# Attention and a gated layer on one core: the decay of the first 320 tokens summed by itself, its rows sent ahead of the weights, copies of the preparation given to planned engines, the last tile's end in parts

## The chip, the cores and the metric

One core of one Trainium2 chip. The time is that of the whole program on the device in microseconds (us). The program uses TensorE (PE, matmuls and transposes), ScalarE (ACT), VectorE (DVE), GpSimd (POOL), and SyncE (SP), whose queue issues all DMA transfers.

## The reference

Attention with a forget-gate decay over 8 batches, 8 heads, 576 tokens and a head width of 64, then a layer over the 4608 tokens (512 wide, 1024 inside), all in float32:

```python
scores = scale * np.matmul(q, k.transpose(0, 1, 3, 2))
log_f = np.log(np.clip(f, 0.0001, 1.0))
cum = np.cumsum(log_f, axis=-1)
decay = cum[:, :, :, None] - cum[:, :, None, :]
scores = np.where(causal, -1000000000.0, scores + decay)
attn = np.exp(scores - max); attn = attn / (sum + 1e-09)
x = np.matmul(attn, v)                  # heads side by side: 4608 x 512

h = x @ w_in                            # 512 -> 1024
solu = h * softmax(h)
mu, var = mean(solu), var(solu)
ln = (solu - mu) / np.sqrt(var + 1e-06) * g_ln
out = ln @ w_out                        # 1024 -> 512
```

## The kernel before

Every step is an `op` with an engine, an assumed duration in ns, a due time, a function that emits the instructions, and the keys that it reads and writes. `Plan.schedule` lays all steps out on a clock of its own. On each engine it takes, among the steps that could start within `WAIT` ns of the earliest one, the one that is due first. The instructions are emitted in that order, so every engine's queue has a fixed order. A due time only ranks steps. On that clock a transfer of `kb` takes `kb / 0.25` ns of the wire and ends at `max(t + 1900, wire + 1300)`; eight may be in flight, and one issue takes 620 ns of SyncE.

Where the planner expects TensorE to have nothing to do for over 200 ns before 140 us, the program emits filler matmuls (L742), whose result nobody reads:

```python
for _ in range(int(FILL * (t - busy - 100.0) / (256 * COLUMN))):   # FILL 1.2, COLUMN 0.4525
    nc.tensor.matmul(dst[:, :256], blank[:, :P], blank, start=True, stop=True)
```

Here `t` is where the next step of TensorE is expected and `busy` where the last ended, 3200 ns at the start.

**Attention.** Heads are taken in 32 pairs (8 batches of 4). A pair has five query tiles (64, then 4 x 128 tokens). For each tile and head `scores` multiplies q and k into PSUM, VectorE subtracts the mask and takes the maximum (L508), ScalarE takes the exponential with its sum (L511), VectorE inverts the sums (L519, L520), GpSimd scales (L524), `transposes` turns the tiles on TensorE (L550) and ScalarE copies them to SBUF (L555); `values` multiplies by v (L590). Matmuls run on operands split into a high and a low float32r part. Only the first batch's first 320 tokens ("early" or "native": half 0 of pairs 0 to 3) use plain float32: q and k are loaded as they are, and one row more holds the decay's sums, sent by DMA from `c32`, a piece of tile p_4 (`kz_k<-p`, `ks_k<-p`). Their outputs go from PSUM to `xt` by one ScalarE copy (L608).

**The decay.** f (64 rows of 576) is loaded into tile e, clipped (L298), its logarithm taken (L299), summed by a scan into tile z (L305) and copied into `c32` (L306 to L311). The keys of these copies are called `summed`; loads of pairs 1 to 3, the rows themselves and w_in's chunks 1 to 3 read `summed`, so they are issued behind them. Step L301 loads ScalarE's table for the exponential (due -40). For all other pairs the sums go split in two through DRAM (`c_scratch`, due `C_OUT`).

**Weights.** w_in and w_out come packed in four chunks of 1 MB each. `weights` loads one into a buffer that is still free, unpacks it with ScalarE (L351, L357) and VectorE (L360, L362) into e, z or ptl, and `prepare_w_in` and `prepare_w_out` then make high and low parts: wi_h on ScalarE (L372), wi_l on GpSimd (L373), w_out times g_ln on ScalarE (L389) and its low part on VectorE (L391).

**The layer.** `layer(n)` takes 128 tokens: split x (L624, L625), 24 matmuls by w_in into hps (L629 to L631), maximum (L638), exponential (L639), the weighing and mean (L643 to L646), the square with its sum on ScalarE (L648) and the centring on GpSimd (L652), which both write z; 8 transposes (L665), high and low parts (L667, L668), 24 matmuls by w_out into one bank (L676 to L678), an output copy (L685) and a transfer. The last tile is like the others.

## Time and profile before

| | |
|---|---|
| time, median of 3 runs | 815.35 us (815.05 to 815.91) |
| the profiled execution | 815.81 us, its span 814.0 us |
| TensorE busy | 799.7 us (98%), 4973 matmuls and transposes |
| VectorE busy | 580.6 us (71%) |
| ScalarE busy | 556.7 us (68%) |
| GpSimd busy | 457.3 us (56%) |
| moved by DMA | 106.96 MB, mean 131 GB/s |

Busy times are shares of the span of one execution. Matmuls are pipelined, and the filler matmuls count as busy too, so TensorE's 98% is not work of the reference alone. Due times and the planner's clock are no measured times.

### The profile page before, as it was taken

To read this page: it belongs to the slowest core of one execution; us is meant where nothing else is said; L and a number is where in the kernel's file an instruction comes from. 1 tells how busy PE (TensorE), PEld (TensorE's weight loads), DVE (VectorE), ACT (ScalarE), POOL (GpSimd) and SP (SyncE) were. 2 spreads that over 40 slices of the span, in tenths; PEclk is the share of its full clock that TensorE was granted. 3 is DMA by queue.
4 is the path that set the end of the run, shared out by engine and by line. 5 is a ranking of instruction groups with operands and counts; after the bars stand their busy time and mean duration, and the time that the engine had idled before them with its cause. 6 is when DMAs were issued, how large, how long until landed. Compare 5 with 4: busy or idle time off the path is not lost.

```text
span 814.0 us, 16055 instructions
## 1 busy us (share of the span) xinstructions
PE 799.7 (98%) x4973; PEld 677.2 (83%) x4973; DVE 580.6 (71%) x1847; ACT 556.7 (68%) x1386; POOL 457.3 (56%) x668
## 2 busy tenths in 40 slices
PE   8999999999999999999999999999999999999997
PEld 6767888888888888888888888888888888888885
DVE  3669888897777777777777777777877777764322
ACT  4977777887666776777777777767767776764332
POOL 5466677766656564666665555656654655432320
PEclk9999999999999999999999999999999999999999
DMA  8658778787554445555554445555444554000000
GB/s 300 164 133 246 185 184 204 211 198 182 144 139 111 125 108 133 148 145 137 153 131 110 111 118 148 145 136 142 125 121 125 132 128 100 28 14 14 26 27 26
DMA packets 64069, 106.96 MB, mean 131 GB/s; under 512 B 11184, under 2 KB 25520, under 8 KB 63216
## 3 DMA queue, kind: packets, MB, share of 16 engines
q1 hardware_dynamic: 63984, 105.95, 49.7%
q8 instruction: 39, 0.64, 0.3%
q14 instruction: 46, 0.38, 0.2%
HBM read 39.11 MB, written 10.03 MB: 60 GB/s over the span
## 4 chain that ended last, share of the span: by engine, by line
PE 87%; DVE 7%; ACT 1%; issue 1%; POOL 1%; DMA 1%; SPq 0%; DVEq 0%; POOLq 0%; ACTq 0%
PE ps_o L590 13%; PE ps_t L550 10%; PE ps_o L676 8%; PE hps L629 8%; PE ps_o L677 7%; PE ps_o L678 7%; PE hps L631 7%; PE hps L630 7%; PE ps L503 5%; PE ps L504 5%; PE ps_t L665 3%; PE ps L742 3%; DVE p L508 2%; PE ps_o L742 1%; PE ps L501 1%
## 5 line engine op out<-in xcount | busy, mean ns | idle before, releaser
L524 POOL TENSOR_SCALAR p<-p,ri 64x64 f32<-64x64 f32 (+4 forms) x320 | 170.3, 547 | 138.1 <-DVE ri L520 108.1
L511 ACT ACTIVATE p<-p,nm 128x192 f32<-128x192 f32 (+4 forms) x320 | 179.3, 561 | 77.5 <-DVE nm L508 62.9
L558 DVE TENSOR_TENSOR ptl_f32r<-ps_t,pth_f32r 128x384 fp32r<-128x384 f32 (+3 forms) x272 | 138.2, 519 | 39.5 <-ACT pth_f32r L555 37.9
L508 DVE CUSTOM_DVE_ANT_0 p<-ps,mask 128x192 f32<-128x192 f32 (+4 forms) x320 | 132.2, 424 | 44.9 <-PE ps L504 28.0
L555 ACT CAST pth_f32r<-ps_t 128x384 fp32r<-128x384 f32 (+3 forms) x272 | 119.1, 450 | 44.4 <-PE ps_t L550 40.5
L550 PE MATMUL ps_t<-ident,p 128*128 128x128 f32 x800 | 129.9, 274 | 2.4 <-DVE ptl_f32r L558 1.1
L676 PE MATMUL ps_o<-wo_f32r,zh 128*128 128x512 f32 x288 | 121.8, 423 | 0.3 <-ACT zh L667 0.3
L629 PE MATMUL hps<-wi_h,xh 128*128 128x512 f32 x288 | 121.3, 421 | 0.4 <-DVE e L645 0.4
L550 PEld LDWEIGHTS ps_t<-ident,p 128*128 128x128 f32 x800 | 96.4, 140 | 28.5 <-POOL p L524 4.6
L677 PE MATMUL ps_o<-wo_f32r,zh 128*128 128x512 f32 x288 | 114.1, 396 | 0.0
L678 PE MATMUL ps_o<-wo_f32r,zl 128*128 128x512 f32 x288 | 113.7, 395 | 0.0
L631 PE MATMUL hps<-wi_h,xl 128*128 128x512 f32 x288 | 113.6, 394 | 0.0
L630 PE MATMUL hps<-wi_l,xh 128*128 128x512 f32 x288 | 113.6, 394 | 0.0
L503 PE MATMUL ps<-ks_f32r,qs_f32r 128*64 128x64 f32 (+2 forms) x360 | 110.6, 314 | 2.2 <-DVE nm L508 1.9
L504 PE MATMUL ps<-kz_f32r,qz 128*64 128x64 f32 (+2 forms) x360 | 103.7, 295 | 0.0
L590 PE MATMUL ps_o<-pth_f32r,vs_f32r 128*128 128x256 f32 (+1 forms) x368 | 93.7, 267 | 0.0
L652 POOL TENSOR_SCALAR z<-e,st 128x1024 f32<-128x1024 f32 x36 | 42.7, 1185 | 73.5 <-ACT z L648 73.3
L668 DVE TENSOR_TENSOR zl<-ps_t,zh 128x512 fp32r<-128x512 f32 x72 | 47.6, 687 | 50.8 <-ACT zh L667 50.4
L625 POOL TENSOR_TENSOR xl<-xt,xh 128x512 fp32r<-128x512 f32 x36 | 46.5, 1292 | 63.4 <-ACT xh L624 63.1
L503 PEld LDWEIGHTS ps<-ks_f32r,qs_f32r 128*128 128x128 f32 (+1 forms) x360 | 64.8, 180 | 13.8 <-DVE nm L508 6.9
L590 PE MATMUL ps_o<-ptl_f32r,vs_f32r 128*64 128x256 f32 (+1 forms) x368 | 72.0, 262 | 0.0
L590 PEld LDWEIGHTS ps_o<-pth_f32r,vs_f32r 128*128 128x128 f32 x368 | 68.9, 188 | 1.5
(110 smaller groups left out, 1608.6 us busy)
## 6 DMA issues: line engine op xcount, KB each, us to landing
raw<-in_qk_dram SPq DMA_DIRECT2D x64, 288.0 KB
ks_f32r<-hi SPq DMA_DIRECT2D x128, 144.0 KB
raw<-in_v_dram SPq DMA_DIRECT2D x32, 288.0 KB
kz_f32r<-raw SPq DMA_DIRECT2D x64, 144.0 KB
out_dram<-y SPq DMA_DIRECT2D x36, 256.0 KB
qs_f32r<-hi SPq DMA_DIRECT2D x56, 144.0 KB
qs_f32r<-raw SPq DMA_DIRECT2D x56, 144.0 KB
qz<-hi SPq DMA_DIRECT2D x56, 80.0 KB
```

What stands on the lines that cost most here:

```text
L503: nc.tensor.matmul(dst, qs(p)[:, h, q0:q0 + nq], ks(p)[:, h, cols], start=True, stop=False)
L508: op(DVE, R_NS[i], at + 0.5, lambda a=a, e=e, key=key: nc.vector.tensor_tensor_reduce(pr[:, a:e], ps[plan.place[key]][:nq, :e - a], mask[: ...
L511: op(ACT, E_NS[i], at + 1.3, lambda: nc.scalar.activation(pr, pr, AF.Exp, bias=x, scale=-1.0, accum_out=sm[m][i][:nq, h, 0:1]), [("nm", m, ...
L524: op(POOL, N_NS[i], at + 2.8, lambda g=g, pg=pg: nc.gpsimd.tensor_scalar(pg, pg, r_[:, g:g + 1], 1.0, ALU.mult, ALU.mult), [("ri", m, i)], ...
L550: nc.tensor.transpose(tp[:, s, :], pt[i][:, k * P:(k + 1) * P], ident)
L590: nc.tensor.matmul(o[:mm, a:w], vv, mv, start=(j == 0 and x == 0), stop=(j == order[-1] and x == 0))
L629: nc.tensor.matmul(hps[:, sl], xh[:, c, :], wi_h[:, c, sl], start=(c == 0), stop=False)
L630: nc.tensor.matmul(hps[:, sl], xh[:, c, :], wi_l[:, c, sl], start=False, stop=False)
L631: nc.tensor.matmul(hps[:, sl], xl[:, c, :], wi_h[:, c, sl], start=False, stop=(c == NCC - 1))
L676: nc.tensor.matmul(o, zh[a][:, j], wo(0, k), start=(k == 0), stop=False)
L677: nc.tensor.matmul(o, zh[a][:, j], wo(1, k), start=False, stop=False)
L678: nc.tensor.matmul(o, zl[a][:, j], wo(0, k), start=False, stop=(k == NFC - 1))
```

## The change

- The clip and the logarithm run in two pieces, tokens 0 to 319 and 320 to 575. A scan of the first piece into tile y fills `c32`; the scan of all 576 tokens into z follows (due -30) for `c_scratch`.
- w_in's chunk 0 is due at -98, right after f. w_out's chunks read `summed`, so they are issued behind the rows' copies.
- A helper `copied` puts a copy on an engine from a table: wi_h (all ScalarE), the product of w_out and g_ln (VectorE four, GpSimd two, ScalarE two), the transposed copies of the native pairs (VectorE for pair 1), their output copies (five of eight on VectorE). wi_l of chunk 2 goes to VectorE.
- The last tile: its square writes a part of p_4 and no longer z, VectorE does the centring in two halves of 512 columns, and the product by w_out runs in two halves of 256 columns with an output copy and a transfer each, the four low-part matmuls of a group behind the eight high-part ones.
- New due times, `WAIT` from (30, 90, 60, 180, 30) to (0, 90, 60, 60, 0) for (PE, ACT, DVE, POOL, SP).

```diff
+WI_H, WI_L, WO_H, WO_L = (1, 1, 1, 1), (3, 3, 2, 3), (2, 3, 2, 2, 3, 1, 1, 2), (2, 2, 2, 2, 2, 2, 2, 2)
+P_32, X_32 = (1, 2, 1, 1), (2, 2, 2, 2, 1, 1, 1, 2)
-WAIT = (30.0, 90.0, 60.0, 180.0, 30.0)
+WAIT = (0.0, 90.0, 60.0, 60.0, 0.0)
-PAIR = 23.6
-C_OUT = 19.0
-START = 89.0
-HALF = ((4.2, 1.6), (34.8, -12.5))
-W_IN, W_OUT, LOAD = (8.2, 2.2), (39.4, 2.1), (6.8, 5.2)
-W_DMA = (-1.8, 1.6)
+PAIR = 23.79
+C_OUT = 24.8
+START = 89.4
+HALF = ((3.1, 1.8), (29.8, -13.0))
+W_IN, W_OUT, LOAD = (8.4, 2.1), (28.9, 4.9), (8.9, 6.4)
+W_DMA = (3.2, 0.5)
-FIRST = 107.8
-STAGES = (5.2, 5.4, 2.7, 19.0, 10.3)
+FIRST = 106.0
+STAGES = (6.6, 3.8, 2.5, 19.8, 10.3)
...
+    def copied(eng, ns, due, out_, in_, reads, writes, scale=1.0, clear=(), port=True):
+
+        def fn():
+            if eng == ACT:
+                nc.scalar.activation(now(out_), now(in_), AF.Copy, scale=scale)
+            else:
+                (nc.vector if eng == DVE else nc.gpsimd).tensor_scalar(now(out_), now(in_), scale, 1.0, ALU.mult, ALU.mult)
+        op(eng, ns[eng], due, fn, reads, writes, clear=clear, port=port and eng == DVE)
...
-    op(DVE, 450, -99, lambda: nc.vector.tensor_scalar(ft, ft, 1.0e-4, 1.0, ALU.max, ALU.min), writes=[("e",)], port=True)
-    op(ACT, 800, -99, lambda: nc.scalar.activation(ft, ft, AF.Ln), writes=[("e",)])
-    op(ACT, 1500, -40, lambda: nc.scalar.activation(nhalf, ft[:, 0:1], AF.Exp), reads=[("e",)], writes=[("table",)])
+    for n, sl in enumerate((slice(0, HALF_S), slice(HALF_S, S))):
+        op(DVE, (330, 300)[n], -99 + n, lambda sl=sl: nc.vector.tensor_scalar(ft[:, sl], ft[:, sl], 1.0e-4, 1.0, ALU.max, ALU.min),
+           reads=[("e",)], writes=[("f", n)], port=True)
+        op(ACT, (560, 490)[n], -99 + n, lambda sl=sl: nc.scalar.activation(ft[:, sl], ft[:, sl], AF.Ln), reads=[("e",)], writes=[("f", n)])
+    op(ACT, 1500, -40, lambda: nc.scalar.activation(nhalf, ft[:, 0:1], AF.Exp), reads=[("e",), ("f", 0), ("f", 1)], writes=[("table",)])
...
-    op(DVE, 1380, -99, lambda: nc.vector.tensor_tensor_scan(zero, ft, zero, 0.0, ALU.add, ALU.add), reads=[("e",)], writes=[("z",)], port=True)
-    op(DVE, 300, -99, lambda: nc.vector.tensor_copy(c32[:, HALF_S:], zero[:H, :HALF_S]), reads=[("z",)], writes=[("p", 4)], port=True)
-    op(ACT, 260, -99, lambda: nc.scalar.copy(c32[:, 0:P], zero[:H, q_lo(2):q_lo(3)]), reads=[("z",)], writes=[("p", 4, "c")])
+    first = yt[:B * H, :HALF_S]
+    op(DVE, 830, -99, lambda: nc.vector.tensor_tensor_scan(first, ft[:, :HALF_S], zero[:, :HALF_S], 0.0, ALU.add, ALU.add),
+       reads=[("e",), ("f", 0), ("z",)], writes=[("y",)], port=True)
+    op(DVE, 1380, -30, lambda: nc.vector.tensor_tensor_scan(zero, ft, zero, 0.0, ALU.add, ALU.add),
+       reads=[("e",), ("f", 0), ("f", 1)], writes=[("z",)], port=True)
+    op(DVE, 300, -99, lambda: nc.vector.tensor_copy(c32[:, HALF_S:], first[:H]), reads=[("y",)], writes=[("p", 4)], port=True)
+    op(ACT, 260, -99, lambda: nc.scalar.copy(c32[:, 0:P], first[:H, q_lo(2):q_lo(3)]), reads=[("y",)], writes=[("p", 4, "c")])
...
-        dma(due + W_DMA[n // NCC], t, src..., reads=first, writes=tk)
+        dma(due + W_DMA[n // NCC] if n else -98, t, src..., reads=first, writes=tk)
...
-        op(ACT, 1050, due, lambda: nc.scalar.copy(wi_h[:, c, :], w), reads=[wk], writes=[("wi", c)])
-        op(POOL, 2360, due, lambda: nc.gpsimd.tensor_tensor(wi_l[:, c, :], w, wi_h[:, c, :].bitcast(F32), ALU.subtract),
-           reads=[wk, ("wi", c)], writes=[("wil", c)])
+        copied(WI_H[c], {ACT: 1050, DVE: 690, POOL: 1130}, due, wi_h[:, c, :], w, [wk], [("wi", c)])
+        op(WI_L[c], 2360 if WI_L[c] == POOL else 1170, due, lambda: (nc.gpsimd if WI_L[c] == POOL else nc.vector).tensor_tensor(
+            wi_l[:, c, :], w, wi_h[:, c, :].bitcast(F32), ALU.subtract), reads=[wk, ("wi", c)], writes=[("wil", c)], port=True)
...
-        weights(w_out[c], NCC + c, due, t, tk, w, wk)
+        weights(w_out[c], NCC + c, due, t, tk, w, wk, summed)
...
-            op(ACT, 600, due, lambda r=r, k=k: nc.scalar.activation(wo(0, k), w[:, r], AF.Copy, scale=g_sb[:, k:k + 1]),
-               reads=[("g",), wk], writes=[("wo", k)])
+            copied(WO_H[k], {ACT: 600, DVE: 400, POOL: 620}, due, lambda k=k: wo(0, k), w[:, r], [("g",), wk], [("wo", k)], scale=g_sb[:, k:k + 1])
...
-        op(ACT, 60 + 0.81 * n, at + 0.4, lambda: nc.scalar.copy(th(), ps_t[plan.place[key]][:, :cnt, :nq]),
-           [key], [("pth", i, g)], clear=to)
+        copied(P_32[p] if native else ACT, {ACT: 60 + 0.81 * n, DVE: 68 + 1.045 * n}, at + 0.4, th,
+               lambda: ps_t[plan.place[key]][:, :cnt, :nq], [key], [("pth", i, g)], clear=to, port=False)
...
-            op(ACT, 160 + 0.9 * w, at + 1.5, lambda: nc.scalar.copy(xo, ps_o[plan.place[key]][:D, :w]), [key], [(*xk, h)], clear=[xk])
+            copied(X_32[2 * p + h], {ACT: 160 + 0.9 * w, DVE: 68 + 1.045 * w}, at + 1.5, xo, lambda: ps_o[plan.place[key]][:D, :w],
+                   [key], [(*xk, h)], clear=[xk], port=False)
...
+        last = (n + 1) * P == NT
+        sq, sk = (pt[4][:, :DFF], ("p", 4)) if last else (zt, ("z",))
+        if last:
+            for a in range(2):
+                op(DVE, 360, at, lambda a=a: centre(nc.vector, slice(512 * a, 512 * a + 512)), [("e",), ("st", n % 2)], [("z", a)],
+                   clear=[("z",)], port=True)
+        else:
+            op(POOL, 1200, at, lambda: centre(nc.gpsimd), [("e",), ("st", n % 2)], [("z",)])
...
+        if last:
+            for b in range(2):
+                ok, cols = ("o", "y", n, b), slice(256 * b, 256 * b + 256)
+                ...
+                for a in range(2):
+                    for x in range(2):
+                        for k in range(4 * a, 4 * a + 4):
+                            op(PE, (2 - x) * 256 * COLUMN + 4, at + 3.0 * b + 0.1 * k, lambda k=k, x=x, product=product: product(k, x),
+                               [(("zh", "zl")[x], a), (("wo", k), ("wol", k))[x]] if x else [("zh", a), ("wo", k), ("wol", k)], [ok],
+                               take=ok if k == 0 and x == 0 else None)
+                op(ACT, 360, at + 3.0 * b, ...)            # y columns of this half
+                dma(at + 3.0 * b, out[n * P:(n + 1) * P, cols], yt[:, cols], 128, reads=[("y", b)])
+            return
```

The due times of the pairs' steps (`DUE` and `EARLY`) are new too; they have the same form.

## Rows read from the trace of the kernel before

**Rows 1.** Windows of one call; us and instructions of each engine busy

```profile
18.70:50.00 31.30, 31.30 (x205) 21.45 (x204) 18.50 (x82) 27.24 (x76) 17.65 (x26) 1.00 0.57 151
60.00:80.00 20.00, 18.85 (x128) 15.38 (x127) 19.29 (x43) 14.93 (x30) 12.31 (x15) 1.00 0.89 264
200.00:400.00 200.00, 199.69 (x1244) 173.12 (x1243) 150.87 (x500) 142.08 (x364) 121.24 (x174) 1.00 0.52 131
```

**Rows 2.** Windows of the filler matmuls (L742) alone

```profile
0.00:10.00 10.00, 6.58 (x45) 5.27 (x46) 1.00 0.62 204
10.00:18.70 8.70, 8.70 (x81) 7.63 (x79) 1.00 1.02 407
18.70:130.00 111.30, 31.13 (x242) 22.57 (x241) 1.00 0.70 186
```

**Rows 3.** Timeline 0 to 20 us: start, duration, instruction

```profile
0.72 0.57 SPq L289 DMA_DIRECT2D e<-in_f_dram  x1
...
3.39 0.62 DVE L298 TENSOR_SCALAR e<-e 64x576 f32<-64x576 f32 x1 [1.95 <-DMA e<-in_f_dram]
...
3.42 15.39 PE L742 MATMUL ps<-ident 128*128 128x256 bf16 x124 [3.42 <-POOL ident masks.py:199]
...
4.40 0.58 SPq L289 DMA_DIRECT2D wo_raw<-in_w_in_dram  x1
...
4.75 1.28 ACT L301 ACT_TABLE_LOAD   x1
...
5.03 0.43 SPq L289 DMA_DIRECT2D ptl_raw<-in_w_out_dram  x1
5.51 0.60 SPq L289 DMA_DIRECT2D xt<-in_w_out_dram  x1
...
6.15 0.29 ACT L307 COPY p<-z 8x128 f32<-8x128 f32 x1
...
6.79 1.24 SPq L289 DMA_DIRECT2D kz_k<-p  x2
...
9.63 1.14 ACT L351 ACTIVATE e<-wo_raw 128x1024 f32<-128x1024 f32 x1 [2.61 <-DMA wo_raw<-in_w_in_dram]
...
18.74 0.45 PE L501 MATMUL ps<-kz_k,qs_q 65*64 65x64 f32 x4
```

**Rows 4.** Waits of the DMA queue, 9 to 15 us: total, times, longest

```profile
SPq L289 <- DMA xt<-in_w_out_dram: 2.2, 1, 2.2
```

**Rows 5.** Line L501 up to 30 us: durations, first and last start

```profile
L501 PEldq EVENT_SEMAPHORE  x6: 51/51/51, 16.7 to 26.2; - x6
```

**Rows 6.** ScalarE's groups up to 80 us: busy, mean ns

```profile
L555 ACT COPY pth_f<-ps_t 128x384 f32<-128x384 f32 (+2 forms) x16 | 6.0, 376 | 1.3 <-PE ps_t L550 1.3
...
L608 ACT COPY xt<-ps_o 64x320 f32<-64x320 f32 x8 | 3.3, 415 | 3.8 <-PE ps_o L590 3.8
```

**Rows 7.** Line L391: ns min/median/max, first and last start

```profile
L391 DVE SCALAR_TENSOR_TENSOR wo_f32r<-z,g_sb,wo_f32r x4: 747/1018/1855, 57.6 to 75.2; 128x512 fp32r<-128x512 f32 x4
```

**Rows 8.** Timeline of the last 15 us

```profile
799.91 0.15 DVE L646 TENSOR_SCALAR st<-st 128x1 f32<-128x1 f32 x1
...
800.45 0.40 PE L677 MATMUL ps_o<-wo_f32r,zh 128*128 128x512 f32 x1
...
800.69 0.39 PE L678 MATMUL ps_o<-wo_f32r,zl 128*128 128x512 f32 x1
...
801.44 1.12 POOL L652 TENSOR_SCALAR z<-e,st 128x1024 f32<-128x1024 f32 x1 [10.02 <-ACT z L648]
...
802.61 1.09 PE L665 MATMUL ps_t<-ident,z 128*128 128x128 f32 x8 [1.53 <-POOL z L652]
...
803.36 1.07 ACT L667 CAST zh<-ps_t 128x512 fp32r<-128x512 f32 x2 [1.42 <-PE ps_t L665]
...
804.00 0.50 PE L676 MATMUL ps_o<-wo_f32r,zh 128*128 128x512 f32 x1 [0.29 <-ACT zh L667]
...
810.29 0.69 ACT L685 ACTIVATE y<-ps_o,st 128x512 f32<-128x512 f32 x1 [5.86 <-PE ps_o L678]
```

More of the change, by code (lines that the diff above doesn't have):

```diff
@@ L309, in backwards @@
+    op(DVE, 300, -99, lambda: nc.vector.tensor_copy(c32[:, HALF_S:], first[:H]), reads=[("y",)], writes=[("p", 4)], port=True)
+    op(ACT, 260, -99, lambda: nc.scalar.copy(c32[:, 0:P], first[:H, q_lo(2):q_lo(3)]), reads=[("y",)], writes=[("p", 4, "c")])
     def backwards():
-        nc.vector.tensor_copy(c32[:, P:2 * P], zero[:H, q_lo(1):q_lo(2)])
-        nc.vector.tensor_copy(c32[:, 2 * P:HALF_S], zero[:H, :64])
-    op(DVE, 330, -98, backwards, reads=[("z",)], writes=[("p", 4, "d")], port=True)
+        nc.vector.tensor_copy(c32[:, P:2 * P], first[:H, q_lo(1):q_lo(2)])
+        nc.vector.tensor_copy(c32[:, 2 * P:HALF_S], first[:H, :64])
@@ L313, in tile_kernel @@
+    op(DVE, 330, -98, backwards, reads=[("y",)], writes=[("p", 4, "d")], port=True)
     summed = [("p", 4), ("p", 4, "c"), ("p", 4, "d")]
@@ L345, in words @@
             return now(t).rearrange("p c (n t) -> p c n t", t=2)[:, :, :, x]
-        dma(due + W_DMA[n // NCC], t, src.bitcast(I32).rearrange("p (c n) -> p c n", n=512), 712 if tk[0][0] != "xt" else 940, reads=first, writes=tk)
+        dma(due + W_DMA[n // NCC] if n else -98, t, src.bitcast(I32).rearrange("p (c n) -> p c n", n=512), 712 if tk[0][0] != "xt" else 940, reads=first, writes=tk)
         w = w.rearrange("p (c n) -> p c n", c=4)
@@ L647, in layer, with centre @@
         op(DVE, 1780, at, weigh, [("h",)], [("st", n % 2), ("e",)])
[L648 to L653 removed]
+        last = (n + 1) * P == NT
+        sq, sk = (pt[4][:, :DFF], ("p", 4)) if last else (zt, ("z",))
+        op(ACT, 1145, at, lambda: nc.scalar.activation(sq, et, AF.Square, bias=s[:, 4:5], scale=1.0, accum_out=s[:, 5:6]),
+           [("e",), ("st", n % 2)], [sk, ("st5", n % 2)])
+        def centre(eng, cols=slice(0, DFF)):
+            eng.tensor_scalar(zt[:, cols], et[:, cols], s[:, 4:5], 1.0, ALU.add, ALU.mult)
+        if last:
[4 more added lines that the diff above has]
+            op(POOL, 1200, at, lambda: centre(nc.gpsimd), [("e",), ("st", n % 2)], [("z",)])
         def deviation():
@@ L665, in turn @@
                     nc.tensor.transpose(ps_t[plan.place[key]][:, k, :], zt[:, (4 * a + k) * P:(4 * a + k + 1) * P], ident)
-            op(PE, 4 * TRANSPOSE, at + 0.3 * a, turn, [("z",)], [key], take=key, clear=[("zh", a), ("zl", a)])
+            op(PE, 4 * TRANSPOSE, at + 0.3 * a, turn, [("z", a) if last else ("z",)], [key], take=key, clear=[("zh", a), ("zl", a)])
             op(ACT, 470, at + 0.5, lambda a=a, key=key: nc.scalar.copy(zh[a], ps_t[plan.place[key]]), [key], [("zh", a)])
@@ L678, in product_out, with product @@
             nc.tensor.matmul(o, zl[a][:, j], wo(0, k), start=False, stop=(k == NFC - 1))
+        if last:
+            for b in range(2):
+                ok, cols = ("o", "y", n, b), slice(256 * b, 256 * b + 256)
+                def product(k, x, ok=ok, cols=cols):
+                    o = ps_o[plan.place[ok]][:, :256]
+                    a, j = divmod(k, 4)
+                    if x == 0:
+                        nc.tensor.matmul(o, zh[a][:, j], wo(0, k)[:, cols], start=(k == 0), stop=False)
+                        nc.tensor.matmul(o, zh[a][:, j], wo(1, k)[:, cols], start=False, stop=False)
+                    else:
+                        nc.tensor.matmul(o, zl[a][:, j], wo(0, k)[:, cols], start=False, stop=(k == NFC - 1))
+                for a in range(2):
[4 more added lines that the diff above has]
+                               take=ok if k == 0 and x == 0 else None)
+                op(ACT, 360, at + 3.0 * b, lambda ok=ok, cols=cols: nc.scalar.activation(
+                    yt[:, cols], ps_o[plan.place[ok]][:, :256], AF.Copy, scale=s[:, 7:8]), [ok, ("st7", n % 2)], [("y", b)], clear=[("y",)])
+                dma(at + 3.0 * b, out[n * P:(n + 1) * P, cols], yt[:, cols], 128, reads=[("y", b)])
+            return
         for k in range(NFC):
```

9 lines of the change are left out of this document (2 added, 7 removed).

## The prediction

> **What bounds the kernel now.** I read the windows first. From 200 to 400 us TensorE is busy 199.69 of 200 us [rows 1]: in the steady part it sets the pace, and other engines have a quarter of their time free. So the change can win only where TensorE does work that is not the reference's, or waits. The filler matmuls of line 742 show where that is [rows 2]: 6.58 and 8.70 us before the first score, 31.13 us between it and 130 us. Some 46 us of filler stand in the preparation; the reader is to see that 15 of them come before any work at all, and that from 18.7 to 50 us ScalarE is busy 27.24 of 31.30 us, from 60 to 80 us VectorE 19.29 of 20 [rows 1].
>
> Then the timeline of the first 19 us [rows 3]. The first score (L501) starts at 18.74 us. It needs the row of decay sums, which SyncE issues at 6.79. Ahead of it on the queue lie one megabyte of w_in (4.40) and two of w_out (5.03 and 5.51); SyncE itself later stood 2.2 us until the second w_out transfer (xt) had landed [rows 4]. The rows, behind those transfers, cannot have come much earlier. But TensorE's sequencer passed a semaphore for L501 at 16.7 us [rows 5], 2 us before the matmul ran: what stood in the way at the end were the filler matmuls, which are instructions in order. Their number is written into the program from where the planner expects the first score.
>
> **The start, step by step.** The halves first. The clip (0.62 us for 576 columns), the logarithm (0.74, from the clip's end to the table load's start at 4.75) and the scan each shrink by 320/576 on the path. With the clip at 0.35 and a half's logarithm at 0.4, the logarithms of both halves end at about 4.6 us. Behind them the planner puts the table load (1.28) and its small exponential, since the decay's copy on ScalarE (L307) is not ready then and this engine waits 90 ns at most. So that copy starts near 6.15, where it starts today, and the rows are issued at about 6.5 instead of 6.79 [rows 3]: the early half by itself brings 0.3 us.
>
> Then the order of transfers. w_out now reads `summed`, so it is issued after the rows; w_in chunk 0 goes second (due -98), near 1.35 instead of 4.40. It took 5.2 us from issue to use today (4.40 to 9.63), so it is done by 6.6; q and k of the first pair, now issued behind it from about 2.5 on, are 320 KB and follow before the rows. The added wait holds SyncE from about 5.0 to 6.5, where w_out is the only thing that it could have sent; w_out's own users come due at 28.9 and later, so this wait costs 0. Nothing large is then ahead of the rows. A small transfer by itself: f, issued at 0.72, is clipped at 3.39, 2.67 us later. The two rows of the first pair so land by 6.5 + 0.6 + 2.7 = 9.8 us [rows 3].
>
> Then the fillers. Their number follows from the planner's arithmetic in the code (a transfer ends 1.9 us after its issue or 1.3 us after its bytes, whichever is later, with 4 ns for each count of kb: 712 for w_in and the first w_out, 940 for the second). By it the first score stood at 15.27 us of its clock, which gives int(1.2 x (15270 - 3200 - 100) / 115.84) = 124 fillers; the timeline has 124 by its count before L501, so I read the rule rightly [rows 3]. Now: f, first clip, both logarithms and the table end at 5.6, the copy at 5.87, the row is issued at 6.06 and there at 7.96, the score at 8.15, so 50 fillers. These are counts, not times; the time of one I take from the trace: 45 run by 10.0 us, and 81 more take 8.70, 0.107 us each, at a granted clock of 1.00 [rows 2]. Five more give 10.54. So the fillers still end after the data (9.8), and the first score moves from 18.74 to about 10.55: **-8.2 us**. Bounds: if the copy does go ahead of the table load, the data decides near 9.5 (-9.2); if the rows find w_in late, 12 (-6.7).
>
> **What the rest of the preparation gives or takes.** The w_in chunk 0 that ScalarE unpacked from 9.63 on in dead time now lands near 6.6, but et is read by the full scan. That scan takes at most 1.4 us (today it lies between 4.75 and 6.15 [rows 3]) and follows the copies, which end near 5.8, so it lasts until about 7.1, the unpacking starts there, and about 1 us of it (one cast of the wi_h kind) falls beside the first scores. Against that ScalarE loses five of eight output copies (0.415 us each, 2.1 us) and the transposed copies of one pair (four at a mean of 0.376, 1.5 us) [rows 6], and six of eight w_out copies, planned at 0.6 each. ScalarE was 87% busy from 18.7 to 50, so 1 to 4 us less of its work could show there; VectorE, which gets most of it, had 12.8 us free in the same stretch [rows 1]. From 60 to 80 VectorE has 0.7 us free, so what falls there is paid in full. The w_out chunks come due about ten us earlier (28.9 instead of 39.4), out of that crowd. I take **-1.0**, between -6 (a fifth of the 31 us of filler after 18.7 goes [rows 2]) and +6 (next paragraph).
>
> The w_out copies on VectorE read and write SBUF. The nearest row is L391, which has two SBUF inputs: 0.747 us at best, 1.018 in the median, 1.855 at worst for the same instruction [rows 7]. Five such steps move to VectorE (four copies and one difference of w_in); at the spread of that row, 1.1 us each, they are 5.5 us dearer in the worst case, and nothing is added in the best. I take it inside the -1.0.
> The Trainium skill ("GPSIMD Engine Reference", 1. Specifications) says why the same instruction could have two prices: GpSimd's SBUF interfaces are shared with VectorE, and contend with its instructions of two SBUF inputs or a two-port mode. That rule speaks against moving these copies; by it the sum would be 5.5 us worse, by the row's lowest duration unchanged.
>
> The new due times and waits (TensorE and SyncE 30 to 0, GpSimd 180 to 60) reorder the steady part too. When TensorE is the last to be free, every ready step has the same earliest time, so a wait of 0 still picks by due time; I take 0, with bounds of 3 us either way. The c_scratch rows come later (due 24.8 for 19.0), and behind them only pairs 0 to 3's second halves wait, which start tens of us later: 0.
>
> **The tail.** Today the last tile's mean is ready at 799.91 + 0.15; GpSimd starts the centring at 801.44 because both it and the square write z, and the transposes start at 802.61 [rows 8]. After the change the square writes elsewhere and VectorE centres in halves. One half costs at most the clip's 0.62 us (576 columns [rows 3]) so it is done by 800.7. TensorE is busy with the tile before until 800.69 + 0.39 = 801.08: the transposes start there, 1.5 us earlier. ScalarE then has the square, until about 801.4 (GpSimd started behind it), and the former tile's output (0.69), so the cast that today starts at 803.36 starts at 801.8 to 802.1, 1.3 to 1.5 earlier [rows 8]. The products by halves are the same columns, ordered so that zl is not needed at once. Today 24 products lie between 804.00 and the copy at 810.29, 6.29 us; at the 0.24 us from one to the next before it (800.45 to 800.69) they would need 5.8, so some 0.4 is a wait that the new order can hide; the last output copy is half as wide: 0.69 goes to about 0.45 [rows 8]. Sum 1.4 + 0.4 + 0.2 = **-2.0**, bounds -1.2 and -2.6. The first half's transfer is issued while the second half's products run: 0.
>
> **Sum.** -8.2 - 1.0 - 2.0 = -11.2 us. The profiled execution took 815.81 us (span 814.0 and 1.8 around it), 0.46 above the median of the three. 815.81 - 11.2 = 804.6; on the median's scale 804.2. I say **804.4 us**. That an earlier start is kept to the end is read from the steady part [rows 1]: from 200 us on at the latest TensorE had almost no slack: what comes earlier at its start comes earlier at its end.
>
> **Rivals.**
> A, the forecast: the earlier start is passed on. 804.4, itself 801.5 to 807.5. Chance 0.52.
> B, more: earlier w_out chunks and the freed ScalarE also take out some 6 us of the 31 us of later filler, not 1: 799.4. For it speaks ScalarE's 87%; against it that VectorE, near full from 60 to 80, gets the work [rows 1, 2]. 0.16.
> C, given back: VectorE (moved copies, and its slow state in L391's row) becomes the bound up to 80 us, +5.5: 810. For it: 19.29 of 20 us, and 1.855 against 0.747 [rows 1, 7]. Against: 12.8 us free before 50. By the contention rule of the Trainium skill's page named above this is the case to expect. 0.19.
> D, the change doesn't do what it says: the rows still come late, or as many fillers are emitted, so the start stays at 18.7 and only the tail is won: 813.3. Against: the count of fillers follows from the new order. 0.05.
> E, slower: the new order in the steady part makes TensorE wait in front of groups more often. Today 1244 matmuls take 199.69 us [rows 1], 0.1605 each. Over the 720 us after 80 us, 11.2 us are 1.6%: from 0.1630 us a matmul on this decides; at 1.8%, +13.0, it gives 817.2. For it: the wait and due changes reach the whole program. Against: nothing but order changes there, and what is ready is still taken by due time. 0.08.
>
> **Range and chances.** 799 to 811: it takes in A, B's middle, C, and leaves out D, E and the far end of B. A measurement of this kernel tells 0.2%, 1.6 us, from no change. Faster: A, B, C and most of D, 0.89. Same 0.03 (D's rest). Slower: E, 0.08.
>
> **What would show it.** Right: 50 fillers and then L501 at 10 to 11 us; w_in second on the queue and w_out behind the rows; VectorE's full stretch (60 to 80 today) about 8 us earlier and less full; L665 of the last tile 1.5 us behind the former product or less. Wrong: L501 early, but VectorE full from 45 to 70 us and fillers in greater number there (C); fewer than 20 us of filler after the first score (B); under 1225 matmuls in the 200 us of the steady part (E).

## The result, and the profile after

The kernel after took 805.46 us (median of 4 runs, 804.66 to 806.33) against 815.53 (815.05 to 815.91) for the kernel before beside it: ratio 0.9865, 95% interval 0.9851 to 0.9879. The total was forecast at 804.4. Its profiled execution took 804.66 us, 11.15 less than that of before; the forecast sum was -11.2. The total fits, its terms do not, and the traces say so at once.

To see where the time came from I gave each matmul of the reference a weight in us (its columns at 2.4 GHz, four times that for the native float32 ones; transposes 0.105 us; fillers nothing; 692.8 us in all) and noted when so much of it had been started. The weights are for counting and are not measured times: four native products of 320 columns, 2.13 us by weight, took 1.24 us at 24.93 us. All kernels are counted alike. "Work" stands for that sum in all that follows. Times in us of the profiled executions, worked out from the traces:

```
work           1      10      25      40      60      80     100     200     400     675
before      19.5    31.4    47.1    64.9    92.5   120.0   145.2   259.9   482.5   787.8
after       11.7    32.1    47.9    66.5    95.1   118.2   141.2   255.2   475.8   778.7
after-bef.  -7.8    +0.7    +0.8    +1.6    +2.7    -1.8    -4.1    -4.8    -6.8    -9.1
```

So the start brought 7.8 us and all of it was gone by 10 us of work. The preparation, from 1 to 100 us of work, is 3.7 us *longer* than before; between 100 and 675 another 5.0 us are won, and the tail brings the last 2.1.

**The start.** Timeline of the kernel after, 0 to 12 us (start, duration, instruction), against [rows 3]:

```profile
1.35 0.56 SPq L301 DMA_DIRECT2D wo_raw<-in_w_in_dram  x1
...
3.42 7.94 PE L793 MATMUL ps<-ident 128*128 128x256 bf16 x53 [3.42 <-POOL ident masks.py:199]
...
3.72 1.28 ACT L314 ACT_TABLE_LOAD   x1 [3.72 <-DMA e<-in_f_dram]
...
5.02 0.78 ACT L314 ACTIVATE e<-e 64x320 f32<-64x320 f32 x2
...
7.21 0.28 ACT L326 COPY p<-y 8x128 f32<-8x128 f32 x1
...
7.52 1.22 SPq L301 DMA_DIRECT2D kz_k<-p  x2
...
11.29 1.06 PE L519 MATMUL ps<-kz_k,qs_q 65*64 65x64 f32 x4
```

The first score moved from 18.74 to 11.29, -7.45. It sits right behind 53 fillers (L793 here), so fillers still set it. But the rows are issued at 7.52, *later* than the 6.79 of before: the table load of the logarithm (1.28 us) used to run at 0.72, in dead time, and now runs at 3.72, released by f's transfer. The new logarithm reads f's key besides that of the clip; that this second key is what holds the load is read from the code and was not tried by itself. The Trainium skill ("ScalarE: Activation LUTs", What ACT_TABLE_LOAD costs) gives 1283 ns for such a load; the trace agrees, 1.28 us.

**What follows it.** Windows (duration; us and instructions of PE, PEld, DVE, ACT, POOL; granted clock; DMA share; GB/s); those from 18.7, 60 and 200 us stand against [rows 1]. The last line is of e11, a kernel described below, from 25 to 30 us:

```profile
18.70:50.00 31.30, 26.75 (x158) 18.25 (x156) 22.60 (x79) 22.32 (x57) 16.53 (x26) 0.84 0.61 181
25.00:30.00 5.00, 1.18 (x5) 0.50 (x4) 3.42 (x14) 5.00 (x14) 2.65 (x3) 0.80 0.77 185
30.00:35.00 5.00, 4.27 (x9) 1.47 (x9) 3.06 (x4) 1.19 (x2) 1.51 (x3) 0.50 0.77 252
35.00:40.00 5.00, 5.00 (x28) 3.97 (x28) 3.26 (x16) 3.22 (x9) 1.65 (x3) 0.68 0.78 263
50.00:60.00 10.00, 10.00 (x67) 6.33 (x65) 9.79 (x19) 6.01 (x14) 7.34 (x9) 1.00 0.88 266
60.00:80.00 20.00, 19.78 (x124) 15.22 (x124) 17.61 (x43) 13.84 (x29) 13.02 (x16) 1.00 0.75 214
200.00:400.00 200.00, 200.00 (x1249) 174.38 (x1248) 152.38 (x494) 143.90 (x362) 120.99 (x170) 1.00 0.53 135
400.00:600.00 200.00, 200.00 (x1260) 174.87 (x1259) 152.34 (x500) 145.16 (x369) 119.00 (x170) 1.00 0.51 130
...
25.00:30.00 5.00, 4.77 (x27) 2.39 (x25) 3.97 (x17) 4.37 (x12) 3.18 (x4) 1.00 0.78 189
```

The chain of waits of the kernel after, 24 to 31 us (start, duration, what), and TensorE's timeline there:

```profile
...
24.32 1.16 ACT e L370
25.48 0.88 ACT p L529 x4
26.36 0.95 ACT wi_h L295
27.31 1.09 ACT p L529 x4
28.40 0.27 ACT pth_f L295
28.66 1.06 ACT ps_o L376 x2
29.73 0.42 ACT pth_f L295
30.14 0.58 issue
...
```

```profile
24.93 1.24 PE L519 MATMUL ps<-kz_k,qs_q 65*128 65x320 f32 x4
30.73 4.02 PE L608 MATMUL ps_o<-pth_f,raw 64*64 64x320 f32 x8 [4.55 <-ACT pth_f L295]
```

From 25 to 30 us ScalarE is busy 5.00 of 5.00: the unpacking of w_in's chunks (L370, L376, the copy into wi_h) lies in its queue among the exponentials and the transposed copies, and TensorE has 1.18 us of work: its next products wait 4.55 us for the copy `pth_f`. In the next 5 us the granted clock is 0.50 (the lower level, 1.2 GHz), and nine matmuls take 4.27 us. This wait is half of where the head start goes. From 1 to 10 us of work the kernel after needs 20.4 us and before 11.9, 8.5 us more: 4.6 of them are this idle time, and 3.7 are filler (9.74 us of L793 from 11.7 to 32.1 us, 6.02 of L742 from 19.5 to 31.4 in before). The lower clock behind it cost no time against before: from 10 to 25 us of work both need some 15.7 us, the kernel after with 3.45 us of filler and before with 6.14, at a clock of 1.00.

**The fillers**, windows of L793 alone, against [rows 2]:

```profile
0.00:10.00 10.00, 6.58 (x43) 5.14 (x44) 1.00 0.48 153
10.00:18.70 8.70, 6.65 (x57) 5.18 (x54) 1.00 0.99 333
18.70:130.00 111.30, 22.66 (x182) 17.14 (x181) 0.95 0.73 200
```

After 18.7 us 22.66 us of filler are left of 31.13, so 8.5 fewer, but 6.65 now stand between 10 and 18.7 us: 5.3 of these behind the first score. Of the 3.7 us that the preparation is longer from 1 to 100 us of work, TensorE's idle time is +3.1 (5.1 for 1.9), filler -2.7 (27.95 for 30.64), and the rest, some 3.3, is its work taking longer, at the lower clock or less closely packed.

**The tail**, timeline of the kernel after against [rows 8]:

```profile
790.84 0.15 DVE L665 TENSOR_SCALAR st<-st 128x1 f32<-128x1 f32 x1
...
791.11 0.88 DVE L674 TENSOR_SCALAR z<-e,st 128x512 f32<-128x512 f32 x2
...
791.62 0.39 PE L705 MATMUL ps_o<-wo_f32r,zl 128*128 128x512 f32 x1
...
791.86 1.03 PE L692 MATMUL ps_t<-ident,z 128*128 128x128 f32 x8
...
799.46 0.47 ACT L727 ACTIVATE y<-ps_o,st 128x256 f32<-128x256 f32 x1 [2.26 <-PE ps_o L719]
```

The transposes follow the former tile's last product by 0.24 us (1.92 before, 800.69 to 802.61). From the start of that product to the span's end it is 802.8 - 791.62 = 11.18 us, against 814.0 - 800.69 = 13.3: -2.1, forecast -2.0. Behind 675 us of work all nine kernels with the new tail, here and below, need 24.0 to 24.1 us, the five with the old one 26.2 to 27.5.

**The dearer copies.** Lines L409 (L391 before, [rows 7]) and L297 (the moved copies) of the kernel after: ns min/median/max, first and last start:

```profile
L409 DVE SCALAR_TENSOR_TENSOR wo_f32r<-z,g_sb,wo_f32r x4: 735/841/1137, 52.2 to 70.5; 128x512 fp32r<-128x512 f32 x4
L409 DVE SCALAR_TENSOR_TENSOR wo_f32r<-ptl_w,g_sb,wo_f32r x4: 750/886/1083, 56.6 to 81.5; 128x512 fp32r<-128x512 f32 x4
...
L297 DVE TENSOR_SCALAR wo_f32r<-ptl_w,g_sb x3: 479/481/939, 56.1 to 77.6; 128x512 fp32r<-128x512 f32 x3
```

One of the four w_out copies on VectorE took twice its time (0.939 for 0.48), not all five steps as the bound allowed (5.5 us); the fifth, the difference of w_in, took 1.22 us at 31.87 and has no other of its shape beside it. So two prices exist, but here the worst of L409 is 1.137 where L391 reached 1.855. By the rule of the Trainium skill named in the prediction ("GPSIMD Engine Reference", 1. Specifications) GpSimd would be the reason; the trace agrees in part: of the twelve steps of 128x512, the five above 0.9 us all ran beside a GpSimd instruction, but so did two of L409 that took 0.735 and 0.748, at 69.8 and 70.5 us.

### The profile page after: what moved, and what is told of

Its sections match the earlier page's. It is cut to its first block, busy times and chain, and to the rows that moved or that the text cites. A ratio compares the mean times of both kernels' runs of the same rounds, so it can differ in the third digit from the quotient of the medians.

```text
span 802.8 us, 15984 instructions
## 1 busy us (share of the span) xinstructions
PE 790.1 (98%) x4924; PEld 675.7 (84%) x4924; DVE 590.5 (74%) x1865; ACT 554.5 (69%) x1373; POOL 459.9 (57%) x668
## 4 chain that ended last, share of the span: by engine, by line
PE 93%; DVE 2%; ACT 1%; DMA 1%; issue 1%; POOL 1%; SPq 0%; POOLq 0%; DVEq 0%; ACTq 0%
PE ps_o L608 15%; PE ps_t L568 11%; PE hps L648 8%; PE hps L649 8%; PE hps L650 8%; PE ps_o L703 8%; PE ps_o L704 8%; PE ps_o L705 8%; PE ps L521 6%; PE ps L522 6%; PE ps_t L692 4%; PE ps L793 2%; PE ps_t L793 1%; PE ps L519 1%; PE ps_o L793 1%
## 5 line engine op out<-in xcount | busy, mean ns | idle before, releaser
L542 POOL TENSOR_SCALAR p<-p,ri 64x64 f32<-64x64 f32 (+4 forms) x320 | 174.3, 558 | 123.4 <-DVE ri L538 53.4
L529 ACT ACTIVATE p<-p,nm 128x320 f32<-128x320 f32 (+4 forms) x320 | 178.9, 560 | 72.8 <-DVE nm L526 68.3
L526 DVE CUSTOM_DVE_ANT_0 p<-ps,mask 128x320 f32<-128x320 f32 (+4 forms) x320 | 132.7, 423 | 35.2 <-PE ps L522 21.5
L295 ACT ACTIVATE pth_f32r<-ps_t 128x384 fp32r<-128x384 f32 (+3 forms) x272 | 121.8, 461 | 34.3 <-PE ps_t L568 31.2
L703 PE MATMUL ps_o<-wo_f32r,zh 128*128 128x512 f32 x280 | 118.5, 423 | 0.0
L568 PEld LDWEIGHTS ps_t<-ident,p 128*128 128x128 f32 x800 | 98.4, 140 | 23.5 <-issue 2.9
L704 PE MATMUL ps_o<-wo_f32r,zh 128*128 128x512 f32 x280 | 110.9, 396 | 0.0
L705 PE MATMUL ps_o<-wo_f32r,zl 128*128 128x512 f32 x280 | 110.2, 394 | 0.0
L521 PE MATMUL ps<-ks_f32r,qs_f32r 128*64 128x64 f32 (+2 forms) x360 | 107.5, 309 | 0.3 <-DVE nm L526 0.2
L608 PE MATMUL ps_o<-pth_f32r,vs_f32r 128*128 128x128 f32 (+1 forms) x368 | 96.1, 272 | 0.0
L608 PE MATMUL ps_o<-ptl_f32r,vs_f32r 128*64 128x128 f32 (+1 forms) x368 | 71.2, 262 | 0.2 <-DVE ri L537 0.2
L608 PEld LDWEIGHTS ps_o<-pth_f32r,vs_f32r 128*128 128x128 f32 x368 | 69.3, 189 | 1.6
```

The lines of the kernel that those rows point to most:

```text
L521: nc.tensor.matmul(dst, qs(p)[:, h, q0:q0 + nq], ks(p)[:, h, cols], start=True, stop=False)
L529: op(ACT, E_NS[i], at + 1.3, lambda: nc.scalar.activation(pr, pr, AF.Exp, bias=x, scale=-1.0, accum_out=sm[m][i][:nq, h, 0:1]), [("nm", m, ...
L542: op(POOL, N_NS[i], at + 2.8, lambda g=g, pg=pg: nc.gpsimd.tensor_scalar(pg, pg, r_[:, g:g + 1], 1.0, ALU.mult, ALU.mult), [("ri", m, i)], ...
L568: nc.tensor.transpose(tp[:, s, :], pt[i][:, k * P:(k + 1) * P], ident)
L608: nc.tensor.matmul(o[:mm, a:w], vv, mv, start=(j == 0 and x == 0), stop=(j == order[-1] and x == 0))
L703: nc.tensor.matmul(o, zh[a][:, j], wo(0, k), start=(k == 0), stop=False)
```

## The experiments

Each ratio is to runs of the kernel before beside it on the same chip (medians of 816.0 to 817.5 us); the kernel after has 0.9865. 0.1% is 0.8 us. The work table, in us of the profiled executions (of e1, e3, e4 and e7 the text gives what is used). Each line is one execution, and its time can lie off the median of its runs: that of e6 is the fastest of four (804.45, median 807.61), that of e4 the fastest of ten (813.03, 815.05), that of e7 the slowest of ten (817.93, 815.11). So a difference of 2 us between two lines is not shown by the table alone.

```
work                  1      10      25      40      60      80     100     200     675
after              11.7    32.1    47.9    66.5    95.1   118.2   141.2   255.2   778.7
e2 late start      18.6    38.9    55.7    75.6   105.0   129.2   152.2   266.2   790.7
e5 clock held      12.3    32.0    45.1    65.7    94.1   121.4   144.4   258.3   783.3
e6 12 fewer         9.8    30.7    46.5    65.1    93.6   116.8   139.8   253.8   778.5
e8 start only      11.6    27.0    42.7    67.2    94.0   123.6   152.3   268.7   795.3
e9 old engines     11.4    31.8    51.4    69.8    96.5   121.8   148.6   267.5   790.9
e10 old steady     12.2    32.5    48.5    67.0    92.9   123.4   148.0   262.2   789.5
e11 old prep dues  12.0    27.2    45.2    63.8    90.4   116.4   140.9   257.9   783.0
e12 start + dues   12.5    32.8    49.6    68.1    95.2   121.2   148.2   264.8   791.5
before             19.5    31.4    47.1    64.9    92.5   120.0   145.2   259.9   787.8
```

### One part alone: tail, steady order, start

**e1, the tail alone**: the kernel before with the new `layer`.

```diff
+        last = (n + 1) * P == NT
+        sq, sk = (pt[4][:, :DFF], ("p", 4)) if last else (zt, ("z",))
...
```

> The kernel before with only the last tile changed (square into another tile, centring by VectorE in halves, product by halves). The sum's tail term says 2.0 us less: 813.5. The trace of the change reads 2.15 us less from the former tile's last product to the end (11.18 for 13.33). A rival that puts the whole gain into the tail would say 804.

Measured: ratio 0.996 (0.9945 to 0.9974), -3.3 us, interval -2.1 to -4.5. At 675 us of work its profiled run stands 0.4 us behind before, and its span is 1.8 us shorter, so its tail gives -2.2. By the trace the tail's -2.0 stands; the medians say about 1 us more, and why is open.

**e4, the steady due times and waits alone**, in the kernel before.

```diff
-WAIT = (30.0, 90.0, 60.0, 180.0, 30.0)
+WAIT = (0.0, 90.0, 60.0, 60.0, 0.0)
...
-PAIR = 23.6
+PAIR = 23.79
...
```

> The kernel before with the changed kernel's due times of the later pairs and layers (DUE, PAIR, START, FIRST, STAGES) and its waits, and nothing else. The two traces say that from 200 to 700 us the change gains some 4 to 5 us on the steady work: if that comes from the order there, 4 to 6 us less, 810. The forecast counted the reorder at 0: 815.5. If an order planned with other parts of the preparation is worse, slower than 815.5.

Measured: 0.9977 (0.9964 to 0.999), -1.9 us. Windows of this kernel:

```profile
200.00:400.00 200.00, 200.00 (x1258) 174.84 (x1257) 152.99 (x506) 144.54 (x370) 119.84 (x172) 1.00 0.52 133
400.00:600.00 200.00, 200.00 (x1257) 174.60 (x1255) 152.67 (x495) 144.22 (x366) 117.86 (x168) 1.00 0.52 133
```

In these 400 us 2515 matmuls run, 2509 in the kernel after. Between 200 and 675 us of work it needs 523.7 us, the kernel after 523.6, before 527.9. The steady order by itself is worth 4.2 us there in these two executions; before that it is slower, by 1.4 us at 200 us of work. Over all kernels here the same stretch takes 523.5 to 525.2 us in the eight kernels with the new steady part and 526.6 to 528.3 in the six with the old one: the two groups don't overlap, and their means differ by 3.0 us.

**e8, the early start alone**: the halves, the first scan, w_in ahead and w_out behind the rows, in the kernel before; engines, due times, waits and tail old.

```diff
+    for n, sl in enumerate((slice(0, HALF_S), slice(HALF_S, S))):
...
-        dma(due + W_DMA[n // NCC], t, ...
+        dma(due + W_DMA[n // NCC] if n else -98, t, ...
...
-        weights(w_out[c], NCC + c, due, t, tk, w, wk)
+        weights(w_out[c], NCC + c, due, t, tk, w, wk, summed)
```

> The kernel before with the start alone changed: halves of clip, logarithm and scan, w_in chunk 0 second, w_out behind the rows; old due times, old waits, old engines of the copies, old tail. If the earlier start is passed on by itself: first score near 11.3, 7 us less, ratio 0.991. If the head start needs the new due times and engines, because ScalarE is full from there on: less than 3 us, ratio 0.996 or more.

Measured: **slower**, 1.0105 (1.0087 to 1.0123), +8.6 us. The score is as early as in the kernel after, the run is 4.4 us ahead of before at 25 us of work, and by 100 it is 7 us behind. From 25 to 40 us of work it needs 24.5 us for 17.8; another 4.8 are lost between 40 and 100. Chain of waits and a window of this kernel where it turns:

```profile
58.74 3.88 DMA ks_f32r<-hi
62.67 0.41 POOL hi L446
63.16 1.04 POOL raw L449
64.20 1.26 POOL p L530 x2
```

```profile
60.00:70.00 10.00, 9.89 (x75) 8.44 (x73) 5.19 (x9) 3.64 (x7) 6.01 (x7) 1.00 0.76 189
```

Between 60 and 70 us VectorE and ScalarE are half idle: the chain waits for a pair's operands, whose transfers and GpSimd splits stand in a fixed order among w_out's transfers (its third chunk is issued at 52.0 us, its fourth at 68.1). That these are what delays the operands is read from the order and not shown.

### More or less of the start

**e2, the late start**: the kernel after with 69 more fillers ahead of the first score, everything else in its order.

```diff
-for _ in range(int(FILL * (t - busy - 100.0) / (256 * COLUMN))):
+for _ in range(int(FILL * (t - busy - 100.0) / (256 * COLUMN)) + (69 if busy == 3200.0 else 0)):
```

> The changed kernel with 69 filler matmuls more ahead of the first score, so that it starts near 18.7 us again, as before the change; order and everything else as in the changed kernel. If the early start is passed on to the end (the forecast's step) the time is that of the changed kernel plus 7.4 us: 812.9. If the head start is gone by 60 us, as the landmarks of the two traces say, it is the changed kernel's time plus 0 to 2 us: 805.5 to 807.5.

Measured: 1.001 (0.9997 to 1.0023), +11.8 us over the kernel after for a score 6.9 us later. My theory that the head start is gone by 60 us and therefore worth nothing fell. The delay is 6.9 us up to 10 us of work, 9.1 at 40, 11 from 80 on: the third chunk of w_out is issued at 57.01 for 49.23, and its 8.03 us lie in the chain:

```profile
57.01 8.03 DMA ptl_raw<-in_w_out_dram
```

**e6**, the kernel after with 12 fewer fillers there (`- (12 if busy == 3200.0 else 0)`), and **e7**, the kernel before with 30 fewer.

> The changed kernel with 12 filler matmuls fewer ahead of the first score. The rows of the first pair are there by 9.8 us, so the first score moves from 11.29 to about 10.0. If fillers are the last thing that holds it and the start is passed on: 1.3 us less, ratio 0.985. If the data holds it: 11.29 and 0.9865.

> The kernel before with 30 filler matmuls fewer ahead of the first score and nothing else. If its score was held by fillers and not by the rows, it starts at 15.5 to 16.7 us instead of 18.74, and passed on this is 2 to 3 us less: ratio 0.997. If the rows behind w_out set it (theory of the transfers alone) the score stays at 18.7 and the ratio at 1.000.

Measured: 0.9897 (0.988 to 0.9915) and 0.9991 (0.9981 to 1.0001). e6 scores at 9.41 us, right behind its 41 fillers, which shows that the rows are there by then; its profiled execution is still 1.4 us ahead of the kernel after at 200 us of work and 0.2 at the end. That execution is the fastest of e6; by the ratios e6 is 2.6 us slower than the kernel after, and the intervals don't meet. So nothing is gained, and why something is lost is open. e7 scores at 15.44, 3.3 us earlier and now held by the rows' transfer, and is level with before at 50 us of work; in its chain stands w_out's third chunk again:

```profile
55.11 9.14 DMA ptl_raw<-in_w_out_dram
```

So 2 to 3 us won at the front by fillers alone are absorbed in either kernel, and a late front isn't: there the whole order behind it moves.

### The stall at 25 to 40 us

**e3 and e5, fillers into the stall** of the kernel after, ahead of the first `values`, in e3 (38 of them) into the bank that this step then takes, in e5 (40) into hps, which is free. The edit of e5:

```diff
+        steps = plan.schedule()
+        first_value = next(o for _, o in steps if o.take and o.take[:3] == ("o", 0, 0))
...
+                if o.take and o.take[:3] == ("o", 0, 0):
+                    for _ in range(40 if o is first_value else 0):
+                        nc.tensor.matmul(hps[:, :256], blank[:, :P], blank, start=True, stop=True)
```

> The changed kernel with 38 filler matmuls where TensorE idled 4.6 us (26.2 to 30.7 us) ahead of the first product with v, after which its clock was at half until 38 us. Order as in the changed kernel. If an earlier end of this stretch is passed on, 2 to 3 us less: 803. If what comes before 60 us is absorbed later, the same within 1 us: 805.5, though the eight products with v take some 2 us instead of 4.

> The changed kernel with 40 filler matmuls into hps, which nobody uses yet, at the place where TensorE idled from 26.2 to 30.7 us. Unlike those of the run before they wait for no bank. If the half clock from 28 to 38 us is a loss that is passed on: the eight products with v take 2 us instead of 4 and the time is 2 to 3 us less than the changed kernel's, 0.983 to 0.984 of before. If it is absorbed: 0.9865.

e3 measured 0.9954 (0.9934 to 0.9974): the unpacking of weights uses that bank, so the fillers waited too, L608 came 5.9 us later (36.66 us), and the kernel ended 7.3 us later. It says nothing on the clock. e5 measured 0.9891 (0.9842 to 0.994), no gain over the kernel after. Its windows:

```profile
25.00:30.00 5.00, 5.00 (x42) 4.24 (x41) 3.46 (x15) 5.00 (x13) 2.10 (x3) 1.00 0.80 194
30.00:35.00 5.00, 4.82 (x31) 2.62 (x29) 4.49 (x11) 2.47 (x8) 2.08 (x3) 1.00 0.67 236
...
110.00:115.00 5.00, 3.99 (x18) 3.54 (x19) 2.13 (x8) 1.75 (x6) 3.21 (x4) 0.66 0.83 229
```

The clock is kept at 1.00 and the run is 2.8 us ahead at 25 us of work; of that 0.8 are left at 40. What this execution loses later is another stall (its chain has `kz_f32r<-raw`, 4.36 us, at 106.8, and the clock falls to 0.66 behind it), so its end says little. But two of e5's four runs had a mean granted clock of 1.000: they took 804.53 and 805.69 us, where the four of the kernel after, at 0.992 to 0.994, took 804.66 to 806.33. A price of 2 to 3 us, as expected, would show there; the stall is real, but most or all of the clock's price is absorbed behind it.

### One part taken back

**e9**, the kernel after with every copy on its old engine; **e10**, with the old steady due times and waits; **e11**, with the old due times of the preparation; **e12**, the kernel of e8 with the new ones.

```diff
# e9
-WI_H, WI_L, WO_H, WO_L = (1, 1, 1, 1), (3, 3, 2, 3), (2, 3, 2, 2, 3, 1, 1, 2), (2, 2, 2, 2, 2, 2, 2, 2)
-P_32, X_32 = (1, 2, 1, 1), (2, 2, 2, 2, 1, 1, 1, 2)
+WI_H, WI_L, WO_H, WO_L = (1, 1, 1, 1), (3, 3, 3, 3), (1, 1, 1, 1, 1, 1, 1, 1), (2, 2, 2, 2, 2, 2, 2, 2)
+P_32, X_32 = (1, 1, 1, 1), (1, 1, 1, 1, 1, 1, 1, 1)
# e10: DUE, PAIR, START, FIRST, STAGES, WAIT of before; e11: EARLY, C_OUT, HALF, W_IN, W_OUT, LOAD, W_DMA of before
...
-W_IN, W_OUT, LOAD = (8.4, 2.1), (28.9, 4.9), (8.9, 6.4)
+W_IN, W_OUT, LOAD = (8.2, 2.2), (39.4, 2.1), (6.8, 5.2)
...
# e12: e8 with these seven of after
```

> The kernel after, with every copy of the preparation back on the engine that it had before: wi_l all on GpSimd, the eight w_out products, the transposed copies and the output copies of the native pairs on ScalarE. Start, order of transfers, due times, waits and tail stay new. Theory 1 (the engine plan is what keeps the early start alive: with the start moved alone ScalarE could not follow): 811 to 816, at least 6 us over the kernel after, and the loss is built up between 25 and 80 us with ScalarE over 90% busy. Theory 2 (VectorE's dearer copies eat what ScalarE is spared; rival C of the forecast in a small form): 804 to 807, within 2 us of the kernel after.

> The kernel after, with the due times of the steady part (DUE, PAIR, START, FIRST, STAGES) and WAIT as before. Theory 1 (the parts add: the steady order by itself brought 1.4 to 1.9 us when put into the kernel before): 806.5 to 807.5. Theory 2 (the early start pays only with the new steady order): over 812. Theory 3 (the forecast: the steady order is worth 0): 804.5 to 806.

> The kernel after, with the due times of the preparation as before (EARLY, HALF, W_IN, W_OUT, LOAD, W_DMA, C_OUT): w_out comes due at 39.4 again and not at 28.9. Theory 1 (the early start alone was slower because w_out's chunks stood at their old due times and landed in the middle of the preparation's work): 812 to 820, with a loss of 6 us or more between 50 and 85 us and the third chunk of w_out issued at 48 us or later. Theory 2 (the engine plan alone carries the early start): 804 to 808.

> The kernel before, with the halves, the first scan, w_in ahead, w_out behind the rows (the run that had the early start alone, 824.4) and in addition the preparation's due times of the kernel after; engines of the copies, steady due times, WAIT and tail as before. Theory 1 (the due times of the preparation turn the early start into a gain): 807 to 811. Theory 2 (the engine plan is needed as well): 814 to 822.

Measured, ratio and cost over the kernel after:

```
e9  old engines      1.0008 (0.9993 to 1.0023)   +11.7 us
e10 old steady part  0.9985 (0.9973 to 0.9997)    +9.8
e11 old prep dues    0.9901 (0.9884 to 0.9919)    +2.9
e12 start + dues     1.0043 (1.0023 to 1.0062)   (+3.5 us over before)
```

e9: theory 1 by its total (its range ended 1 us below), not by its place: from 25 to 80 us ScalarE is busy 39.99 us of 55, not over 90%. 3.5 us are lost up to 25 us of work, where the granted clock stays low longer; windows of this kernel:

```profile
35.00:40.00 5.00, 5.00 (x21) 4.15 (x21) 2.70 (x12) 2.80 (x11) 1.67 (x3) 0.50 0.75 267
40.00:45.00 5.00, 5.00 (x22) 3.22 (x22) 1.55 (x8) 4.22 (x11) 2.91 (x3) 0.56 0.01 4
...
155.00:160.00 5.00, 3.34 (x24) 2.48 (x22) 4.72 (x18) 4.44 (x12) 4.03 (x6) 1.00 0.69 159
160.00:165.00 5.00, 4.41 (x24) 3.94 (x25) 4.67 (x19) 4.66 (x11) 3.71 (x5) 0.66 0.76 224
```

But most of that is made up by 60 us of work, and 11 more are lost between there and 200, with a second stall among them (155 to 165 us, the last two lines). One thing goes with the engines in the kernels with the new start and no filler put in: w_out's fourth chunk is issued at 57.2 to 57.8 us with the new ones (after, e10, e11; 55.8 in e6), at 61.2, 62.9 and 68.1 with the old (e12, e9, e8). I read from it that the spared ScalarE lets the weights come earlier; that this is what the 11 us are is not shown. e10: theory 2; it is 2.2 us ahead of the kernel after at 60 us of work and 7.1 behind at 200, since these due times also rank the second half of the preparation, and 3.6 more go from 200 on, where it runs 1242 and 1248 matmuls in the two windows. e11: neither as put. It is the fastest of the table from 40 to 80 us of work, and w_out's third chunk is issued earlier (45.4), not later, than in the kernel after: theory 1's reason fell. At 100 us of work it is level, at 200 it is 2.7 behind. e12: theory 2; the due times take back 5.1 of the 8.6 us of e8 and not more.

These runs also tell which of the new parts brings the stall at 25 us. All have the early start. At 10 us of work those with the new due times of the preparation and the planner's fillers stand at 32.1 and 32.5 with the new engines (after, e10) and at 31.8 and 32.8 with the old ones (e9, e12); the two with the old due times at 27.2 with the new engines (e11) and 27.0 with the old (e8), with TensorE busy 4.77 and 4.73 us from 25 to 30 us and a clock of 1.00. So the due times put the unpacking ahead of the copies that TensorE waits for, whatever the engines, and with the old ones over 4 us of the head start still stand at 10 us of work. They are lost later: e8 ends slower than before, and e11 behind the kernel after.

## Why the prediction was right, and which steps weren't

**The start's mechanism was right**: fillers set the first score before and after, w_in is second on the queue, w_out behind the rows. Its size was 7.45 (forecast 8.2): 53 fillers for 50. The rows were forecast to be issued at 6.5 and were at 7.52, for the table load that I had not seen would move behind f. It cost nothing here, since fillers end later still (e6). w_out behind the rows was priced at 0, as a wait of SyncE from 5.0 to 6.5; but its first two chunks, issued at 5.03 and 5.51 before, went out only at 29.88 and 30.98, so that 2 MB moved from the dead time into the preparation. No run keeps them in front with the rest new, so what this cost is not shown.

**"What comes earlier at its start comes earlier at its end" failed.** I read it from TensorE's full windows after 200 us, and it holds there; between the start and there stands a stretch with filler and waits in it, where order, transfers and ScalarE decide. The head start was gone at 32 us, some 5 us of it by the new due times, and the same early start with the old engines and due times made the kernel 8.6 us slower (e8). What I called the rest of the preparation, -1.0 with bounds of -6 and +6, came out at +3.7. Rival C had the size of this in its price, 5.5, but not the place: VectorE's dear copies were one of four; the loss began with ScalarE at 25 us. I had expected it to be relieved, and on average it was (22.32 us from 18.7 to 50, 27.24 before), but not in the 5 us where TensorE waited for it. Of my signs, VectorE from 60 to 80 us is less full, 17.61 for 19.29, but from 50 to 60 it has 9.79 of 10, 6.74 before. From 45 to 70 us, the stretch named for rival C, VectorE has 21.64 us of 25 (18.71 before) and fillers 7.94 (7.24): C's sign was there, weakly.

**The steady order, taken at 0 with bounds of 3, brought 5.0** (4.3 of it from 200 us of work on). e4 and e10 show it with and without the other parts: 4.2 and 3.6 us there, and 3.0 over all kernels, so that 1 us of the 4.3 may be the luck of two executions. Rival E feared the other sign; the windows show 1249 and 1260 matmuls for 1244 and 1244, the last of these in the kernel before:

```profile
400.00:600.00 200.00, 198.79 (x1244) 172.32 (x1243) 151.61 (x491) 142.19 (x361) 116.29 (x166) 1.00 0.52 132
```

Idle time carries the smaller part: from 200 to 700 us TensorE was idle 1.7 us before and 0.0 after. The rest is closer packing, and mean times of single forms went both ways (the first score product of 288 columns 320 to 305 ns, `values` of 256 columns 280 to 293). Why this order packs closer is open.

**The tail** was right: -2.1 for -2.0, and e1 agrees.

So +4.7 and -5.0 cancelled, and the forecast of 804.4 was met by luck in these two terms. More is shown by the parts taken back one at a time: they cost 11.7 (engines), 9.8 (steady order) and 2.9 (due times). The start was not taken back but delayed, for 11.8 (e2), and the tail, put in alone, is worth some 2 to 3: together 38 to 39 us where all of them bring 11. Of the three parts put in by themselves, tail, steady order and start, only the tail brings over 2 us; the engines and the due times of the preparation were not put in alone. The parts are one order, and what each is worth hangs on the others. That any change of the planner's inputs redraws the order of the whole preparation is part of these numbers: e9 to e12 each have another order there, and I can't say how much of each figure is the part's own and how much such a redraw. e2, e3, e5, e6 and e7 keep the order, and they say that delays of 6 to 7 us at the front are passed on in full or more, while gains of 2 to 3 us are not passed on.

What was not tried: the halves without the new order of transfers, and the logarithm without its read of f's key, so that the table load goes back to 0.72; e6 speaks against a gain from it alone.

## What to carry to other kernels

A full TensorE at the end of a program says nothing on whether time won at its front arrives: check each stretch between for fillers and waits, and price the stretch with the least slack by what it waits for, transfers and order included. Where engines follow a written order, moving a part of it is a new order of all that stands behind, so measure parts both alone and taken back; if the two disagree, the terms of a sum can't be added. Look at the work done by a time, fillers left out, and not at busy shares, when two schedules are compared.
